# Own buffers for the strided heads, u^T of batch 1 in natural order, and a last step tile by tile

## The chip, the cores and the metric

The kernel runs on one core of one Trainium2 chip. The metric is device time in microseconds of one execution. The engines are PE (TensorE: matmuls and transpositions), DVE (VectorE), ACT (ScalarE), POOL (GpSimd) and SP (SyncE, which here only issues DMAs). ACT and POOL issue DMAs as well.

## The reference

For 8 batches, 8 heads, 576 positions and head size 64, attention is computed with two kinds of masks, and its output goes through a token-mixing and a channel-mixing layer:

```python
mask_local = (rel >= 0) & (rel < 32)                                       # heads 0 to 3
mask_strided = (rel >= 0) & (pos[None, :] % 32 == pos[:, None] % 32)       # heads 4 to 7
x = softmax(where(mask, q @ k.T / 8, -1e9)) @ v      # per head, put together to 576 x 512
u = x + (x.T @ U @ V).T                              # U: 576 x 32, V: 32 x 576
out = u + relu(u @ w_ch1) @ w_ch2                    # 512 -> 2048 -> 512
```

A strided head has 32 residue classes of 18 positions each, so its scores are 32 causal blocks of 18 x 18.

## The kernel before, in words

**The channel mixing sets the frame.** It runs over nine blocks n: the first 512 positions of batches 0 to 7, and a tail block (n = 8) of the last 64 positions of all eight batches. Each block has 16 steps fc over the 2048 inner columns. A step is `gemm1` (12 matmuls of 128 x 512 into one PSUM bank `ph`), then on ACT `gh` (relu) and on DVE `gl` (what rounding left of it), and `gemm2` (for each of four tiles s of 128 positions, two matmuls with `gh` and one with `gl`, into `accs[n]`). gemm2 of a step is issued behind gemm1 of the next step. The four tiles of `accs[n]` lie in two PSUM tiles of two banks each. `finish` adds x to the four tiles on DVE and sends them out. The two operands `uh` and `ul` of the next block are made by `split` from `raw`.

**The next batch's attention is woven in.** While block n runs, a generator `attention(n + 1)` is advanced along the 32 half-steps ("slots") of the block: local pairs of heads on PE (`scores`, `probabilities` with the tile `s_sb`, `transposed` with the tile `PT`, `outputs`), then the token mixing: `mix_t` (tile `ta`, result `tst`), `mix_u`, `mix_tail`, and `transposes`, which turns x on DVE into `bt` and spreads it into `raw` with 32 small DMAs, half issued by SP and half by ACT. From batch 2 on, `strided_heads(b)` computes the strided heads without PE: POOL multiplies (`tmp`), DVE sums (`tensor_reduce`), for the scores `s_st` (27 products and sums), then a softmax, then for the values (27 products and sums). The reduce of a product is traced one product later. `strided_copies` moves the result into x before the second half of `mix_t`.

**Batches 0 and 1 come first**, in `first_attention`: all heads as pairs on PE, the strided ones with positions sorted by residue class. Their output in class order (tile `x`) goes to DRAM through POOL's queue (`far_dma`), and `od_reads` brings it back in natural order into `xg`. u^T of a pair of heads is made by `quarter(b, pr)`: x transposed on PE into `pu`, U^T x into `pm`, V onto it, and for batch 1 copied to `raw`. For the strided pairs (pr 2 and 3) it takes the class order, with U and V sorted alike (`U_c`, `Vc`, `Vc_last`) and five instead of four pieces to transpose. The quarters of batch 1 run during block 0, in the order `ORDER1`.

**The shared buffers.** `att` gives tiles of one tag with `ATT_BUFS` = 5 buffers: `s_sb`, `PT`, `ta`, `h` of mix_tail, batch 1's `x` and `tst`, and also `s_st` and every `tmp` of the strided heads. During the prefix alone a list `ring` of eight pieces of the tiles `late` takes their place. A new tile waits until the one that had its buffer is read out.

**The order on each engine.** The kernel is traced as one program, and a planner orders each engine's instructions beforehand: it plays the program with costs of its own and gives an engine the first traced instruction that is ready. Work that is ready can so run ahead of its place in the program. On the chip each engine follows its order strictly. `tc.issue_after` adds an order on one engine. S0 and S1 give the slots over which the strided heads of a batch are traced.

Of the kernel before, what the change touches and what calls it, by code (L numbers as in the profile page):

```python
# [7 lines left out]
F32 = mybir.dt.float32  # L8
# [5 lines left out]
ALU = mybir.AluOpType  # L14
AX = mybir.AxisListType
NEG = -1.0e9
ATT_BUFS = 5
NSP = 2
N_EARLY = 9
N_LATE = 48  # L20
# [8 lines left out]
A_TAIL = (4, 20, 8)  # L29
S0 = {2: 20, **{b: 32 * (b - 1) - 12 for b in range(3, 8)}}  # L30
S1 = (20, 14)
ORDER0, ORDER1 = (2, 3, 0, 1), (2, 3, 0, 1)
PAIR = 2 * 576 + 18 * 65


# [1 line left out]
def fused_kernel(ctx, tc, pairs, strided, U, V, w_in, masks, eye, out):  # L37
# [67 lines left out]
    mask_l, ident_b = masks_sb[:, 0:320], masks_sb[:, 320:448]  # L105
    U_sb = const.tile([128, 5, R], F32, name="U_sb")
    Vst = const.tile([96, S], F32R, name="Vst")
    U_c = const.tile([128, 5, R], F32, name="U_c")
    Vc_last = const.tile([96, 64], F32R, name="Vc_last")
    uh, ul = (const.tile([128, NDC, 512], F32R, name=name) for name in ("uh", "ul"))  # L110
    raw = const.tile([128, 4, 4, NDC, 32], F32, name="raw")
# [21 lines left out]
    def small_weights():  # L133
        stage = xp.tile([128, 2, 512], I64, name="xg")
        words_in = stage.rearrange("p a x -> p (a x)")
        dma(out=words_in[:, 0:10 * R], in_=U)
        dma(out=words_in[0:R, 10 * R:10 * R + S], in_=V)
        yield
        with tc.issue_after(marks["PT"][0]):
            f = to_f32(words_in, early, 128, 10 * R)  # L140
        nc.scalar.copy(out=U_sb.rearrange("p t r -> p (t r)"), in_=f[:, 0:5 * R])
        nc.scalar.copy(out=U_c.rearrange("p t r -> p (t r)"), in_=f[:, 5 * R:10 * R])
        with tc.issue_after(marks["PT"][0]):
            f = to_f32(words_in[0:R, 10 * R:10 * R + S], att([128, 640], "cu"), R, S)
        nc.scalar.copy(out=Vst[0:32], in_=f)
        nc.scalar.copy(out=Vst[32:64], in_=f)
        nc.vector.tensor_tensor(out=Vst[64:96], in0=f, in1=Vst[0:32].bitcast(F32), op=ALU.subtract)
        yield
        by_class = Vst.bitcast(F32).rearrange("p (j c) -> p c j", j=NCH)
        nc.scalar.copy(out=Vc[:, 0:504].rearrange("p (c j) -> p c j", j=NCH), in_=by_class[:, 0:28])  # L150
        nc.scalar.copy(out=Vc[:, 504:512], in_=by_class[:, 28, 0:8])
        nc.scalar.copy(out=Vc_last[:, 0:10], in_=by_class[:, 28, 8:18])
        nc.scalar.copy(out=Vc_last[:, 10:64].rearrange("p (c j) -> p c j", j=NCH), in_=by_class[:, 29:32])
        yield
# [76 lines left out]
    def early_pair(b, pr, od, last):  # L231

        tb = 64 * (b % 2)
        by_class = pr >= 2
        kT, qT = load_qk(b, pr)
        yield
        vt = load_v(b, pr)
        yield
        before = marks.get("PV", [])
        with tc.issue_after(before[-1]) if before else nullcontext():  # L240
            sp = scores(kT, qT, mask_s if by_class else mask_l)
        s_sb = yield from probabilities(sp)
        load_behind(len(marks["exp"]) - 1, s_sb[0:1, 0, 0, 0:1])
        PT = transposed(s_sb)
        yield
        op = outputs(PT, vt)
        cs = slice(2 * pr * D, 2 * pr * D + 2 * D)
        if by_class:
            x = att5([128, 640], "x").rearrange("p (t x) -> p t x", t=5) if b else \
                early[:, 320 + 640 * (pr - 2):960 + 640 * (pr - 2)].rearrange("p (t x) -> p t x", t=5)  # L250
            main, last_x, p0 = x[:, 0:4, :], x[0:64, 4, :], 0
            normalised(op, x)
        else:
            xg, xt = x_tiles(b)
            main, last_x, p0 = xg[:, :, cs], xt[tb:tb + 64, cs], tb
            normalised(op, main, last_x, tb)
        if by_class:
            oc = 2 * pr * D - 4 * D
            far_dma(out=od[0:512, oc:oc + 2 * D].rearrange("(t p) d -> p t d", p=128), in_=main)
            far_dma(out=od[512:576, oc:oc + 2 * D], in_=last_x)  # L260
        parts[b, pr] = (main, last_x, p0)
        if last:
            od_reads(b, od)
        yield
        if b == 0:
            quarter(b, pr)
            yield

    def quarter(b, pr):

        main, last_x, p0 = parts[b, pr]
        by_class = pr >= 2
        cs = slice(2 * pr * D, 2 * pr * D + 2 * D)
        Um = U_c if by_class else U_sb
        pu = psx2().rearrange("p a x -> p (a x)")
        pm = ps_h.tile([128, 512], F32, name="ph")[0:32, 0:128] if b == 0 else pu[0:32, 640:768]
        lead = x_transposed(pu, [main[:, t, :] for t in range(4)])
        if by_class:
            lead = x_transposed(pu[:, 512:576], [last_x])
        with tc.issue_after(lead):  # L280
            for t in range(4):
                nc.tensor.matmul(pm, Um[:, t, :], main[:, t, :], start=t == 0 and not (b and by_class), stop=False,
                                 skip_group_check=True, tile_position=(0, 0))
            nc.tensor.matmul(pm, Um[p0:p0 + 64, 4, :], last_x, start=False, stop=True, skip_group_check=True,
                             tile_position=(p0, 0))
        if b not in tsts:
            tsts[b] = ap_.tile([96, DM], F32R, name="tst", **({"tag": "att", "bufs": ATT_BUFS} if b else {}))
        tst = tsts[b]
        nc.scalar.copy(out=tst[0:32, cs], in_=pm)
        nc.scalar.copy(out=tst[64:96, cs], in_=pm)  # L290
        nc.vector.tensor_tensor(out=tst[32:64, cs], in0=pm, in1=tst[0:32, cs].bitcast(F32), op=ALU.subtract)
        for c0, n, Vm in ((0, 512, Vc), (512, 64, Vc_last)) if by_class else ((0, 512, Vst),):
            nc.tensor.matmul(pu[:, c0:c0 + n], tst[:, cs], Vm[:, 0:n], start=False, stop=True, skip_group_check=True)
        src = pu[:, 0:512]
        if by_class:
            src = pu[:, 0:S].rearrange("p (c j) -> p j c", j=NCH)[:, 0:16, :]
        if b:
            dst = raw[:, :, :, pr, :]
            nc.scalar.copy(out=dst, in_=src.rearrange("p (s a) x -> p s a x", s=4) if by_class else
                           src.rearrange("p (s a x) -> p s a x", s=4, a=4))  # L300
        else:
            hi, lo = (u[:, pr, :].rearrange("p (j c) -> p j c", c=32) if by_class else u[:, pr, :] for u in (uh, ul))
            one = nc.scalar.copy(out=hi, in_=src)
            two = nc.vector.tensor_tensor(out=lo, in0=src, in1=hi.bitcast(F32), op=ALU.subtract)
            marks["split0"] = (two.ins, one.ins)
# [115 lines left out]
    def strided_heads(b):  # L421
# [3 lines left out]
        with tc.issue_after(marks["gl"][9]):  # L425
            dma(out=st, in_=strided[b - NSP, :, 0:2 * NCH * D])
        yield
        s_st = att([128, NCH, NCH], "s_st")
        nc.gpsimd.memset(s_st, 8.0 * NEG)
        late = []  # L430

# [4 lines left out]
        for i in range(NCH):  # L436
            for j0 in range(0, i + 1, 9):
                n = min(9, i + 1 - j0)
                tmp = att([128, 9, D], "tmp")
                nc.gpsimd.tensor_tensor(out=tmp[:, 0:n], in0=sk[:, j0:j0 + n], in1=sq[:, i:i + 1].broadcast_to([128, n, D]),  # L440
                                        op=ALU.mult)
                late.append(lambda tmp=tmp, n=n, i=i, j0=j0: nc.vector.tensor_reduce(  # L442
                    out=s_st[:, i, j0:j0 + n], in_=tmp[:, 0:n], axis=AX.X, op=ALU.add))
                flush(1)
                yield
# [17 lines left out]
        for i in range(NCH):  # L463
            step = D if i < 9 else D // 2
            for d0 in range(0, D, step):
                tmp = att([128, (i + 1) * step], "tmp")
                tv = tmp.rearrange("p (j d) -> p j d", d=step)
                nc.gpsimd.tensor_tensor(out=tv, in0=sv[:, 0:i + 1, d0:d0 + step],  # L468
                                        in1=s_st[:, i, 0:i + 1].broadcast_to([128, i + 1, step]), op=ALU.mult)
                late.append(lambda tv=tv, i=i, d0=d0, step=step: nc.vector.tensor_reduce(  # L470
                    out=o_st[:, i, d0:d0 + step], in_=tv.rearrange("p j d -> p d j"), axis=AX.X, op=ALU.add))
                flush(1)
                yield
# [184 lines left out]
        marks.setdefault("gl", []).append(low.ins)  # L658
        return gh, gl

    def gemm2(n, fc, gh, gl):
        if fc == 0:
            accs[n] = [ps_acc.tile([128, 2, 512], F32, name="acc") for _ in range(2)]
        for s in range(4):
            cs = slice(128 * s, 128 * s + 128)
            if fc == 0 and n < NSP:
                nc.tensor.matmul(accs[n][s // 2][:, s % 2, :], Vst[:, cs], tsts[n], start=True, stop=False)
# [1 line left out]
                nc.tensor.matmul(accs[n][s // 2][:, s % 2, :], gt[:, cs], w_parts[fc, 1][:, part, :],  # L669
                                 start=(fc == 0 and i == 0 and n >= NSP), stop=(fc == NFC - 1 and i == 2))  # L670

    def finish(n):
        for s in range(4):
            ot = xgs[n][:, s, :]
            nc.vector.tensor_tensor(out=ot, in0=accs[n][s // 2][:, s % 2, :], in1=ot, op=ALU.add)  # L675
            if n == B:
# [62 lines left out]
    for step, (n, fc) in enumerate(steps):  # L739
# [3 lines left out]
        advance(2 * step)  # L743
        if n == 0:
            convert(2 * upto[min(NFC - 1, fc + CLA)])
        if len(pend) > 1:
            item = pend.pop(0)
            gemm2(*item)
            if item[1] == NFC - 1:
                finish(item[0])  # L750
        advance(2 * step + 1)
    while pend:
        gemm2(*pend.pop(0))
    finish(NB - 1)


def _masks():
# [72 lines left out]
```

## Time and profile before

| | us |
|---|---|
| median of 3 runs (lowest to highest) | 940.63 (939.02 to 941.83) |
| profiled execution, its own time | 940.45 |
| its span | 938.7 |
| PE busy in the span | 909.2 |
| DVE, POOL, ACT busy | 561.6, 325.7, 247.2 |

An engine's busy time counts compute instructions. Block 0 begins at about 53 us, behind the first loads and the first heads; blocks 2 to 6 follow each other every 97.3 us. In a row of the timeline stand start, duration, engine, line, operation and tiles (out <- in), and in brackets the idle time before it with what ended it. "ACTq" and "SPq" are DMA issues on those engines. In the tables of windows stand the length of the window, the busy time and count of PE, PEld (weight loads), DVE, ACT and POOL, then the granted clock of PE, the DMA share and GB/s; a window asked for one line has fewer columns.

### The profile page before, as it was taken

The page shows a single profiled execution, that of the slowest core. Times are in us where ns is not written, and L with a number is a line of the kernel's source. Part 1 is how long each engine was busy: PE and PEld are TensorE (multiplying, and loading weights), DVE is VectorE, ACT ScalarE, POOL GpSimd, SP SyncE. Part 2 cuts the span into 40 slices and gives each one's busy share as a digit, 9 for nine tenths or more (in the row PEclk, how much of TensorE's full clock was granted, in tenths as well). Part 3 has the DMA queues.
Part 4 walks back from the last instruction along what each step waited for, and adds up shares of the span by engine and source line. Part 5 has one row for each costly group of instructions (what it writes and reads, how often), then busy time and mean ns, then how long its engine had stood idle before and what let it go on. Part 6 is the DMA issues. An engine that isn't in the chain of part 4 may idle for free.

```text
span 938.7 us, 16860 instructions
## 1 busy us (share of the span) xinstructions
PE 909.2 (97%) x7032; PEld 727.3 (77%) x7032; DVE 561.6 (60%) x907; ACT 247.2 (26%) x485; POOL 325.7 (35%) x374
## 2 busy tenths in 40 slices
PE   5789999999899999999999999999999999999997
PEld 4667888777677778777887788778877888888885
DVE  4679987757786678666776677657764341122111
ACT  4436542115122412151114221421233111121110
POOL 1213018434854385346644565447440000000000
PEclk9999999999989999999999999999999999999999
DMA  9958210200250114101420142013300231001001
GB/s 349 340 193 343 88 62 26 97 1 26 61 180 3 32 41 166 42 1 60 138 72 2 51 157 72 2 51 99 119 2 1 57 112 23 1 1 46 1 0 45
DMA packets 36780, 74.24 MB, mean 79 GB/s; under 512 B 5952, under 2 KB 20672, under 8 KB 34784
## 3 DMA queue, kind: packets, MB, share of 16 engines
q1 hardware_dynamic: 26464, 66.60, 20.1%
q10 hardware_dynamic: 9280, 4.20, 1.9%
q0 software_dynamic: 960, 2.36, 0.8%
q8 instruction: 55, 0.90, 0.4%
q14 instruction: 21, 0.17, 0.1%
HBM read 54.14 MB, written 11.67 MB: 70 GB/s over the span
## 4 chain that ended last, share of the span: by engine, by line
PE 83%; DVE 6%; POOL 5%; DMA 3%; issue 2%; ACT 1%; SPq 0%; DVEq 0%; POOLq 0%
PE acc L669 38%; PE ph L652 37%; POOL tmp L440 5%; DVE st L470 1%; PE px L380 1%; DMA w1a<-in_w_dram 1%; PE px L346 1%; PE px L367 1%; DMA w2a<-in_w_dram 1%; DMA late<-in_pairs_dram 1%; PE px L511 1%; DMA st<-in_strided_dram 1%; DVE gl L657 1%; PE px L534 1%; DVE s_st L442 0%
## 5 line engine op out<-in xcount | busy, mean ns | idle before, releaser
L657 DVE SCALAR_TENSOR_TENSOR gl<-ph,gh 128x512 fp32r<-128x512 f32 x144 | 98.8, 688 | 224.2 <-ACT gh L656 223.6
L652 PE MATMUL ph<-uh,w 128*128 128x512 f32 x648 | 215.0, 392 | 0.0
L656 ACT ACTIVATE gh<-ph 128x512 fp32r<-128x512 f32 x144 | 86.1, 598 | 471.2 <-PE ph L652 388.9
L440 POOL TENSOR_TENSOR tmp<-st 128x576 f32<-128x576 f32 (+6 forms) x162 | 168.7, 1082 | 114.0 <-DMA st<-in_strided_dram 58.3
L468 POOL TENSOR_TENSOR tmp<-st,s_st 128x448 f32<-128x448 f32 (+7 forms) x162 | 136.5, 873 | 183.7 <-DVE st L470 97.5
L669 PE MATMUL acc<-w,gh 128*128 128x512 f32 x648 | 197.6, 393 | 0.0
L470 DVE TENSOR_REDUCE st<-tmp 128x64 f32<-128x64 f32 (+8 forms) x162 | 137.6, 882 | 15.4 <-POOL tmp L468 14.3
L669 PEld LDWEIGHTS acc<-w,gh 128*128 128x128 f32 x648 | 122.2, 189 | 25.6
L652 PEld LDWEIGHTS ph<-uh,w 128*128 128x128 f32 x648 | 121.3, 188 | 26.4 <-issue 0.4
L652 PE MATMUL ph<-ul,w 128*128 128x512 f32 x324 | 126.8, 391 | 0.0
L669 PE MATMUL acc<-w,gl 128*128 128x512 f32 x324 | 122.2, 393 | 2.1 <-DVE gl L657 2.0
L442 DVE TENSOR_REDUCE s_st<-tmp 128x9 f32<-128x576 f32 (+6 forms) x162 | 87.6, 564 | 26.6 <-POOL tmp L440 25.7
L669 PEld LDWEIGHTS acc<-w,gl 128*128 128x128 f32 x324 | 61.4, 189 | 16.7 <-DVE gl L657 3.2
L652 PEld LDWEIGHTS ph<-ul,w 128*128 128x128 f32 x324 | 60.8, 188 | 12.9
L485 ACT COPY xg<-st 32x256 f32<-32x256 f32 x96 | 38.8, 404 | 8.5 <-DVE st L470 7.2
L522 DVE TENSOR_TENSOR ta<-px,ta 32x256 f32<-32x256 f32 x36 | 15.1, 420 | 33.1 <-ACT ta L520 32.3
L675 DVE TENSOR_TENSOR xg<-acc,xg 128x512 f32<-128x512 f32 x36 | 22.9, 681 | 9.3 <-PE acc L669 9.3
L644 DVE TENSOR_TENSOR ul<-raw,uh 128x512 fp32r<-128x512 f32 x32 | 24.7, 800 | 2.7 <-ACT uh L643 2.7
L652 PE MATMUL ph<-uh,w6a 128*128 128x512 f32 x72 | 25.1, 398 | 0.0
L652 PE MATMUL ph<-uh,w0a 128*128 128x512 f32 x72 | 24.8, 403 | 0.0
L652 PE MATMUL ph<-uh,w1a 128*128 128x512 f32 x72 | 24.1, 391 | 0.0
L652 PE MATMUL ph<-uh,w5a 128*128 128x512 f32 x72 | 23.8, 391 | 0.0
(292 smaller groups left out, 1272.4 us busy)
## 6 DMA issues: line engine op xcount, KB each, us to landing
w<-in_w_dram SPq DMA_DIRECT2D x9, 1024.0 KB, 8.6
out_dram<-xg SPq DMA_DIRECT2D x32, 256.0 KB, 2.1
v<-in_pairs_dram SPq DMA_DIRECT2D x12, 585.0 KB, 4.7
st<-in_strided_dram SPq DMA_DIRECT2D x6, 1152.0 KB, 5.6
qk<-in_pairs_dram SPq DMA_DIRECT2D x12, 576.0 KB, 5.1
late<-in_pairs_dram SPq DMA_DIRECT2D x8, 585.0 KB, 8.7
late<-in_pairs_dram SPq DMA_DIRECT2D x8, 576.0 KB, 9.7
raw<-bt SPq DMA_DIRECT2D x112, 32.0 KB, 1.9
```

Of the source, the lines that this page charges most:

```text
L440: nc.gpsimd.tensor_tensor(out=tmp[:, 0:n], in0=sk[:, j0:j0 + n], in1=sq[:, i:i + 1].broadcast_to([128, n, D]), op=ALU.mult)
L442: late.append(lambda tmp=tmp, n=n, i=i, j0=j0: nc.vector.tensor_reduce(out=s_st[:, i, j0:j0 + n], in_=tmp[:, 0:n], axis=AX.X, op=ALU.add))
L468: nc.gpsimd.tensor_tensor(out=tv, in0=sv[:, 0:i + 1, d0:d0 + step], in1=s_st[:, i, 0:i + 1].broadcast_to([128, i + 1, step]), op=ALU.mult)
L470: late.append(lambda tv=tv, i=i, d0=d0, step=step: nc.vector.tensor_reduce(out=o_st[:, i, d0:d0 + step], in_=tv.rearrange("p j d -> p d j" ...
L485: nc.scalar.copy(out=xg[32 * i4:32 * i4 + 32, :, cs], in_=o_st[rows, i4:16:4, :])
L522: nc.vector.tensor_tensor(out=ta, in0=ps_a[32 * j:32 * j + 32, :], in1=ta, op=ALU.add)
L644: nc.vector.tensor_tensor(out=lo, in0=raw[:, :, :, dc, :], in1=hi.bitcast(F32), op=ALU.subtract)
L652: nc.tensor.matmul(ph, w_parts[fc, 0][:, part, 128 * dc:128 * dc + 128], ut[:, dc, :], start=(dc == dcs[0] and i == 0), stop=(dc == dcs[-1 ...
L656: nc.scalar.activation(out=gh, in_=ph, func=AF.Relu)
L657: low = nc.vector.scalar_tensor_tensor(out=gl, in0=ph, scalar=0.0, in1=gh.bitcast(F32), op0=ALU.max, op1=ALU.subtract)
L669: nc.tensor.matmul(accs[n][s // 2][:, s % 2, :], gt[:, cs], w_parts[fc, 1][:, part, :], start=(fc == 0 and i == 0 and n >= NSP), stop=(fc ...
L675: nc.vector.tensor_tensor(out=ot, in0=accs[n][s // 2][:, s % 2, :], in1=ot, op=ALU.add)
```

## The change

Three parts:

1. `s_st` and `tmp` of the strided heads get tags of their own, one buffer for `s_st` and three of 128 x 576 for `tmp`; `ATT_BUFS` goes from 5 to 2. To make room `U_c` moves into a free part of the tile `late[0]`.
2. Batch 1's strided quarters read the natural order (`xg` and the tail tile, as brought back by `od_reads`) with `U_sb` and `Vst`, as the local quarters do, and `ORDER1` puts them last.
3. In the last block the gemm2 of step 14 is held back, and steps 14 and 15 are done together by tiles: tiles 0 and 1 of both steps and their `finish`, then tile 2, then tile 3.

```diff
-ATT_BUFS = 5
+ATT_BUFS = 2
-ORDER0, ORDER1 = (2, 3, 0, 1), (2, 3, 0, 1)
+ORDER0, ORDER1 = (2, 3, 0, 1), (0, 1, 2, 3)
...
-    U_c = const.tile([128, 5, R], F32, name="U_c")
...
-        nc.scalar.copy(out=U_c.rearrange("p t r -> p (t r)"), in_=f[:, 5 * R:10 * R])
+        nc.scalar.copy(out=late[0][:, 1816:1816 + 5 * R], in_=f[:, 5 * R:10 * R])
...
             far_dma(out=od[512:576, oc:oc + 2 * D], in_=last_x)
+            if b:
+                xg, xt = x_tiles(b)
+                main, last_x, p0 = xg[:, :, cs], xt[tb:tb + 64, cs], tb
...
-        by_class = pr >= 2
+        by_class = pr >= 2 and b == 0
-        Um = U_c if by_class else U_sb
+        Um = late[0][:, 1816:1816 + 5 * R].rearrange("p (t r) -> p t r", r=R) if by_class else U_sb
...
-        s_st = att([128, NCH, NCH], "s_st")
+        s_st = ap_.tile([128, NCH, NCH], F32, name="s_st")
...
-                tmp = att([128, 9, D], "tmp")
+                tmp = ap_.tile([128, 9, D], F32, name="tmp", tag="tmp", bufs=3)
...
-                tmp = att([128, (i + 1) * step], "tmp")
-                tv = tmp.rearrange("p (j d) -> p j d", d=step)
+                tmp = ap_.tile([128, 9 * D], F32, name="tmp", tag="tmp", bufs=3)
+                tv = tmp[:, 0:(i + 1) * step].rearrange("p (j d) -> p j d", d=step)
...
-    def gemm2(n, fc, gh, gl):
+    def gemm2(n, fc, gh, gl, tiles=range(4)):
-        for s in range(4):
+        for s in tiles:
...
-    def finish(n):
-        for s in range(4):
+    def finish(n, tiles=range(4)):
+        for s in tiles:
...
-        if len(pend) > 1:
+        if len(pend) > 1 and step + 1 < len(steps):
...
-    while pend:
-        gemm2(*pend.pop(0))
-    finish(NB - 1)
+    for tiles in ((0, 1), (2,), (3,)):
+        for item in pend:
+            gemm2(*item, tiles=tiles)
+        finish(NB - 1, tiles)
```

More of the change, by code (lines that the diff above doesn't have):

```diff
@@ L281, in quarter @@
             for t in range(4):
-                nc.tensor.matmul(pm, Um[:, t, :], main[:, t, :], start=t == 0 and not (b and by_class), stop=False,
+                nc.tensor.matmul(pm, Um[:, t, :], main[:, t, :], start=t == 0, stop=False,
                                  skip_group_check=True, tile_position=(0, 0))
@@ L298, in quarter @@
             dst = raw[:, :, :, pr, :]
-            nc.scalar.copy(out=dst, in_=src.rearrange("p (s a) x -> p s a x", s=4) if by_class else
-                           src.rearrange("p (s a x) -> p s a x", s=4, a=4))
+            nc.scalar.copy(out=dst, in_=src.rearrange("p (s a x) -> p s a x", s=4, a=4))
         else:
```

## The prediction

> **What bounds the kernel now.** I read the page's first part, then the table of windows, then the chain of waits, then each engine's timeline where the windows showed a hole.
>
> ```profile
> PE 909.2 (97%) x7032; PEld 727.3 (77%) x7032; DVE 561.6 (60%) x907; ACT 247.2 (26%) x485; POOL 325.7 (35%) x374
> 250.00:300.00 50.00, 45.48 (x402) 35.37 (x400) 37.23 (x63) 8.59 (x15) 28.20 (x31) 0.93 0.31 101
> 300.00:350.00 50.00, 50.00 (x321) 39.72 (x320) 33.95 (x55) 16.81 (x40) 27.24 (x29) 1.00 0.11 32
> ```
>
> PE is the bound (first busy column). In the middle of the run it has one large hole, 4.52 us in 250 to 300, where the granted clock (third number from the end) is 0.93; the window behind it is full, as are those after. POOL and DVE are never full, so faster strided heads pay only where they close that hole. Its size is seen in the first-layer matmuls that open blocks 1, 2 and 3:
>
> ```profile
> L652 PE MATMUL ph<-uh,w1a x8: 388/389/389, 167.8 to 170.3; 128*128 128x512 f32 x8
> L652 PE MATMUL ph<-uh,w1a x8: 388/389/389, 274.7 to 277.2; 128*128 128x512 f32 x8
> L652 PE MATMUL ph<-uh,w1a x8: 388/389/389, 372.0 to 374.5; 128*128 128x512 f32 x8
> 924.29 2.72 PE ph L652 x12
> ```
>
> Block 2 takes 372.0 - 274.7 = 97.3 us and block 1 takes 106.9, which is 9.6 more. The last row is a step of the chain: twelve matmuls in 2.72, 0.227 each. Block 1 has four matmuls more (V times tst in gemm2), 0.9. So 8.7 us are lost. Where:
>
> ```profile
> 173.14 0.50 PE L669 MATMUL acc<-w0b,gl 128*128 128x512 f32 x1 [0.63 <-DVE gl L657]
> 247.43 0.40 PE L652 MATMUL ph<-uh,w 128*128 128x512 f32 x1
> 247.71 6.33 ACTq L98 DMA_DIRECT2D raw<-bt  x8
> 254.15 0.60 ACT L656 ACTIVATE gh<-ph 128x512 fp32r<-128x512 f32 x1 [11.56 <-DMA raw<-bt]
> 255.93 0.43 PE L340 MATMUL px<-masks_sb 128*128 128x320 bf16 x2 [2.43 <-DVE xt L549]
> 259.81 0.79 PE L669 MATMUL acc<-w,gl 128*128 128x512 f32 x1 [1.98 <-DVE gl L657]
> 256.50:263.30 6.80, 4.82 (x12) 3.31 (x11) 4.19 (x7) 0.60 (x1) 6.80 (x6) 0.50 0.24 58
> 346.73 0.60 ACT L656 ACTIVATE gh<-ph 128x512 fp32r<-128x512 f32 x1 [4.85 <-DMA raw<-bt]
> 346.75 4.61 ACTq L98 DMA_DIRECT2D raw<-bt  x7
> ```
>
> A step's gh is due when its matmuls end, here at 247.83. ACT's queue had eight DMA issues of the transposes ahead of it. They could start only at 247.71, and gh came at 254.15, 6.3 late. Between a step's matmuls and its gemm2 lie one gemm2 and one gemm1, 2 x 2.72 = 5.44 us; less 0.60 for gh and about as much again for gl, some 4.1 are spare. So PE starved, twice, and ran at half clock for 6.8 us (4.82 busy, so 2.4 lost). In block 2 seven such issues start 0.02 behind a gh and hurt nobody: the queue's order is the same, only the transposes of block 1 were late. What made them late is batch 2's strided heads:
>
> ```profile
> 91.64 0.92 POOL L440 TENSOR_TENSOR tmp<-st 128x64 f32<-128x64 f32 x1
> 95.68 0.70 POOL L440 TENSOR_TENSOR tmp<-st 128x128 f32<-128x128 f32 x1 [3.11 <-PE px L284]
> 137.90 23.84 POOL L440 TENSOR_TENSOR tmp<-st 128x192 f32<-128x192 f32 x22 [41.53 <-DVE xt L549]
> 137.85 0.41 DVE L442 TENSOR_REDUCE s_st<-tmp 128x1 f32<-128x64 f32 x2
> 177.54 1.13 POOL L468 TENSOR_TENSOR tmp<-st,s_st 128x64 f32<-128x64 f32 x3 [8.03 <-DVE s_st L459]
> 196.73 0.73 POOL L468 TENSOR_TENSOR tmp<-st,s_st 128x320 f32<-128x320 f32 x1 [10.86 <-DVE st L470]
> 201.97 3.11 POOL L468 TENSOR_TENSOR tmp<-st,s_st 128x352 f32<-128x352 f32 x4 [3.42 <-PE px L367]
> 177.50:230.50 53.00, 53.00 (x472) 41.73 (x470) 33.60 (x49) 15.35 (x35) 23.40 (x28) 1.00 0.01 2
> 228.12 2.35 DVE L470 TENSOR_REDUCE st<-tmp 128x32 f32<-128x576 f32 x2
> 322.82 1.20 DVE L470 TENSOR_REDUCE st<-tmp 128x32 f32<-128x576 f32 x1
> ```
>
> Products wait for things that have nothing to do with strided heads: 95.68 for a quarter's matmul (its tile x), 137.90 for mix_tail's add (its tile h), 201.97 for a transposition (its tile s_sb). That is the shared ring of five. The last reduce ends at 230.47; in block 2 at 324.02, which is 217.1 on block 1's clock (106.9 earlier). Batch 2 is 13.4 us late.
>
> **The change, part by part.**
>
> *Buffers of their own.* No instruction is added. First half (scores): the first reduce runs on DVE at 137.85 although its product was ready at 92.56, so DVE's order, not the buffer, held it; three products instead of two are ahead then, which saves one, about 0.6, and POOL, without a pause from 137.90 to 161.74, remains the limit. I take nothing. Second half (values): it starts at 177.54 behind the softmax, which stays. The window to 230.50 has 33.60 us of DVE and 23.40 of POOL work. Without any gap DVE ends at 211; if half of its 19.4 idle us stay, at 221. So the last reduce comes 9 to 19 us earlier, about where block 2 has it. To save the first starvation the eight issues must end within the spare time, by 247.83 + 4.1 = 251.9, thus begin at 245.6, only 2.1 earlier. So the stall should go. Block 1 then costs 97.3 + 0.9 + the 0.63 wait at 173.14, which is other DVE work and stays: 98.8 for 106.9, a gain of 8.1. Bounds: 8.7 if that wait goes too, 0 if nothing moves.
>
> *Two shared buffers for the rest.* h, batch 1's x and tst, s_sb, PT and ta now share two. Both x are free once written out, ahead of the read at 70.97 below. tst of batch 1 keeps one until gemm2's first step of block 1 is through (the row at 173.14 is in it); the first s_sb of batch 2 is written behind that step, so s_sb and PT find both free. Cost 0; if PT had to wait, the local pair would be late by a step of 5.44. U_c inside late[0]: that tile is kept by later heads anyway, so weight 8's load is not later. 0.
>
> *Quarters from natural order.* Two quarters lose two of ten transposing instructions and a 64-column matmul each.
>
> ```profile
> 80.69 0.47 PE L667 MATMUL acc<-tst,Vst 96*128 96x512 f32 x1 [0.72 <-DVE xt L396]
> 108.09 1.05 PE L316 MATMUL px<-ident,xg 128*128 128x128 f32 x8
> 70.97 2.21 POOL L101 DMA_DIRECT2D xg<-od  x4 [4.96 <-DMA od<-x]
> ```
>
> Eight cost 1.05, so two cost 0.26. The first of the two quarters stood just ahead of a 0.72 wait for DVE and only lengthens it, so I count one: 0.3 (bounds 0 and 0.6). The strided quarters now need what GpSimd's queue reads back from 70.97 on, but as third and fourth of the order they come at 108 or later: 30 us of cover. Without it PE would wait for a DMA of some us.
>
> *Last two steps tile by tile.*
>
> ```profile
> 930.48 0.39 PE L669 MATMUL acc<-w,gl 128*128 128x512 f32 x1
> 931.16 0.61 PE L669 MATMUL acc<-w,gl 128*128 128x512 f32 x2
> 931.58 2.48 DVE L675 TENSOR_TENSOR xg<-acc,xg 128x512 f32<-128x512 f32 x4 [3.21 <-PE acc L669]
> 932.06 0.39 PE L669 MATMUL acc<-w,gl 128*128 128x512 f32 x1
> 932.31 2.76 ACTq L98 DMA_DIRECT2D out_dram<-xg  x4
> DMA to landing us min/median/max: 2.4/3.0/3.4
> ```
>
> Now the four adds run from 931.58 to 934.06. From 927.01 (924.29 + 2.72) the new order does twelve matmuls for tiles 0 and 1 (to 929.73), six for tile 2 (931.09), whose add ends near 931.75, and six for tile 3. The first add now starts when the matmul at 931.16 ends (931.55), not behind the one at 930.48 that ended at 930.87: the wait is for the whole two-bank accumulator. If tile 3's matmuls, in the same accumulator, wait likewise for tile 2's add, they run 931.75 to 933.11 and the last add ends at 933.75, 0.3 earlier. The last rows then leave on empty queues and land as the fastest here do, 2.4 and not 3.4: 1.0 more. I take 1.3. Without that wait the add ends at 933.1 and the gain is 2.0; with the crowded landing it is 0.3.
>
> The Trainium skill's "PSUM — Partial Sum Buffer", section "Summary: rules for kernel authors", says to read PSUM during matmuls from a different bank and to guard by bank; by it tile 3 need not wait, and the sum below would be 930.1 for 930.8. The rows at 930.48 to 931.58 speak for the wait, so I keep it.
>
> Sum, against the profiled execution's 940.45 (span 938.7; the median of the runs is 940.63, 0.18 above): 940.45 - 8.1 - 0.3 - 1.3 = 930.75, say 930.8.
>
> **Rivals.** (a) *The strided heads do not move.* POOL's longest wait in the second half, 10.86, is put down to DVE's reduce, not to a shared tile, and the first reduce lay ready for 45 us. If DVE's planned order is the limit, only the ends pay: 940.45 - 0.3 - 1.3 = 938.9. Against it: the plan places a reduce by when its product can exist, and that hung on the ring.
>
> (b) *Half of the stall stays.* The second group of eight still meets a due gh: one wait of 2.43 and the 2.4 of half clock remain, so 4.8 of 8.1: 940.45 - 3.3 - 1.6 = 935.6. The Trainium skill's "TensorE: Matmul & The Clock Gate", Part 1, has the clock fall to half after an idle window of about 3.4 us; by that rule waits of 2.43 leave it whole and (b) gives 933.2. The row 256.50:263.30 shows 0.50 without so long a wait, so it disagrees.
>
> (c) *Slower: the DMA issues meet gh in later blocks.* Blocks 2 to 6 now escape by 0.02 us (346.73 and 346.75). If reduces that leave DVE sooner move the transposes within the step, eight issues can come just ahead of a due gh in each: 6.33 - 4.1 = 2.2 each at least, 8.7 as in block 1 at most. Two blocks at 8.7, or five at 2.2, eat the gain. At 4 in each of five: 930.8 + 20 = 950.8. Against it: the transposes follow mix_u's matmuls, and PE, full there, runs those at their place in the program however early the heads are.
>
> **How the numbers follow.** Forecast 0.57, (a) 0.14, (b) 0.12, (c) 0.13, slower for a reason that I do not see 0.04. A difference under 0.3% (2.8 us) is about what this measurement cannot tell from none: below 937.8 is faster, forecast and (b), 0.69; (a) is the same, 0.14; slower 0.17. The forecast's own range is 928 (block 1 at 8.7, tail 2.0, quarters 0.6 make 929.2, less the 1 us by which runs differ) to 934 (tail 0.3, block 1 two or three us short). The range for 8 in 10 adds (b) and (a): 928 to 940.5; left out is 0.17.
>
> **What would show it.** Right: w1a of block 2 begins 98 to 99 us after that of block 1; no PE hole in 240 to 265 and granted clock 1.00 there; the last reduce of batch 2 before 222; no product waits for px, h or x; last add near 933.7. Wrong: POOL still waits some 10 us for L470 and the last reduce ends after 228; or PE holes beside ACT's issues in later blocks.

## The result and the profile after

The changed kernel takes 991.12 us (989.60 to 992.36), the kernel before 940.24 (939.02 to 941.83) on the same chip: a ratio of 1.0539, 95% interval 1.0517 to 1.0562, some 50 us slower. The profiled execution of the changed kernel took 990.63, its span is 988.8. Forecast were 930.8. The experiments below ran on several chips, each beside the kernel before, whose median there was 939.83 to 940.84. Of the ten executions of `e9_tmp_ring` one took 1012.63 at a granted clock of 0.854 and is not in its ratio.

From the page after, the busy times and the granted clock in 40 slices (here a slice is 24.7 us):

```profile
PE 928.9 (94%) x7026; PEld 735.9 (74%) x7026; DVE 569.0 (58%) x907; ACT 246.6 (25%) x485; POOL 330.8 (33%) x374
...
PEclk9697899999999999999999999999999999999999
```

PE is busy for 928.9 us where it was 909.2, with nearly the same matmuls (7026 records for 7032): a part of them ran at a lower clock, and the clock is low in the first five slices. So the first loss is ahead of block 1. The matmuls that open blocks 1, 2 and 3 (before: 167.8, 274.7, 372.0):

```profile
L653 PE MATMUL ph<-uh,w1a x8: 388/389/390, 199.7 to 202.2; 128*128 128x512 f32 x8
L653 PE MATMUL ph<-uh,w1a x8: 388/389/389, 303.8 to 306.3; 128*128 128x512 f32 x8
L653 PE MATMUL ph<-uh,w1a x8: 388/389/390, 406.7 to 409.1; 128*128 128x512 f32 x8
```

Prefix and block 0 lose 199.7 - 167.8 = 31.9 us. Block 1 takes 104.1, 2.8 less than before. Block 2 takes 102.9 for 97.3, and blocks 3 to 5 lose about as much each, 21 in all for the four; behind them nothing more is lost. 31.9 - 2.8 + 21 = 50.1, the difference of the spans.

**The first loss.** The instructions of one tile, the products `tmp`, in 20 to 130 us of the changed kernel (count, duration in ns, first and last start):

```profile
L441 POOL TENSOR_TENSOR tmp<-st x27: 313/1254/1777, 24.8 to 61.7; 128x576 f32<-128x576 f32 x11, 128x64 f32<-128x64 f32 x2, 128x128 f32<-128x128 f32 x2, 128x192 f32<-128x192 f32 x2
L443 DVE TENSOR_REDUCE s_st<-tmp x27: 208/601/753, 25.1 to 63.2; 128x9 f32<-128x576 f32 x11, 128x1 f32<-128x64 f32 x2, 128x2 f32<-128x128 f32 x2, 128x3 f32<-128x192 f32 x2
L469 POOL TENSOR_TENSOR tmp<-st,s_st x27: 304/928/1500, 71.5 to 120.4; 128x320 f32<-128x320 f32 x3, 128x384 f32<-128x384 f32 x3, 128x448 f32<-128x448 f32 x3, 128x512 f32<-128x512 f32 x3
L471 DVE TENSOR_REDUCE st<-tmp x27: 220/918/1232, 71.8 to 124.7; 128x32 f32<-128x320 f32 x2, 128x32 f32<-128x352 f32 x2, 128x32 f32<-128x384 f32 x2, 128x32 f32<-128x416 f32 x2
```

All 54 products and 54 sums of batch 2's strided heads now stand between 24.8 and 126, where all but the first two products ran from 137.9 on before, in the middle of batches 0 and 1 and of the weights' conversion. The table of windows from 20 to 165 us, first of the kernel before, then of the changed one:

```profile
20.00:165.00 145.00, 136.74 (x1520) 108.28 (x1521) 118.16 (x186) 65.85 (x107) 44.61 (x66) 0.99 0.50 180
```

```profile
20.00:165.00 145.00, 114.68 (x1375) 87.73 (x1376) 138.73 (x207) 59.78 (x105) 76.44 (x95) 0.86 0.47 171
```

DVE (third busy column) is at 138.73 of 145 us; PE (the first) falls from 136.74 to 114.68.

**The second loss.** Rows of DVE, ACT and PE in block 1 of the changed kernel, and the window behind PE's wait; blocks 2 to 5 repeat them:

```profile
263.09 3.27 DVE L471 TENSOR_REDUCE st<-tmp 128x32 f32<-128x384 f32 x4
266.40 0.42 DVE L523 TENSOR_TENSOR ta<-px,ta 32x256 f32<-32x256 f32 x1
266.74 0.97 DVE L471 TENSOR_REDUCE st<-tmp 128x32 f32<-128x448 f32 x1
267.75 0.42 DVE L523 TENSOR_TENSOR ta<-px,ta 32x256 f32<-32x256 f32 x1
268.10 0.97 DVE L471 TENSOR_REDUCE st<-tmp 128x32 f32<-128x448 f32 x1
269.10 0.43 DVE L523 TENSOR_TENSOR ta<-px,ta 32x256 f32<-32x256 f32 x1
269.46 0.96 DVE L471 TENSOR_REDUCE st<-tmp 128x32 f32<-128x480 f32 x1
270.45 0.69 DVE L658 SCALAR_TENSOR_TENSOR gl<-ph,gh 128x512 fp32r<-128x512 f32 x1
```

```profile
262.77 0.60 ACT L657 ACTIVATE gh<-ph 128x512 fp32r<-128x512 f32 x1 [1.90 <-PE ph L653]
269.56 0.40 ACT L525 CAST tst<-ta 32x256 fp32r<-32x256 f32 x1 [6.20 <-DVE ta L523]
269.99 0.40 ACT L526 CAST tst<-ta 32x256 fp32r<-32x256 f32 x1
270.42 0.60 ACT L657 ACTIVATE gh<-ph 128x512 fp32r<-128x512 f32 x1
```

```profile
271.19 0.50 PE L670 MATMUL acc<-w,gl 128*128 128x512 f32 x1 [1.77 <-DVE gl L658]
```

```profile
271.20:275.50 4.30, 4.26 (x12) 3.09 (x13) 4.27 (x5) 0.00 (x0) 2.92 (x4) 0.65 0.00 0
```

The value sums of the next batch (L471) alternate with mix_t's sums (`ta`). The `gl` that PE waits for is the one of 270.45. Its `gh` is that of 262.77, since no other `gl` stands between the two, and that `gh` came as soon as its matmuls ended. It was done at 263.37, so `gl` stood 7.1 us behind other work in DVE's order, seven value sums (6.2 us) among it. PE waits 1.77; then it runs 4.3 us at a clock of 0.65. The same wait (1.76 or 1.77) comes once in each of blocks 1 to 5.

ACT is held back too: its copies of `tst` wait 6.20 for `ta`, and the `gh` of 270.42 is queued behind them. But that `gh` belongs to the next step, whose `gl` PE takes up at 278.66 without a wait, so here it costs nothing. Over the whole run the waits of ACT for `ta` show how far DVE's order pushed mix_t back, first in the changed kernel, then before:

```profile
ACT tst L525 <- DVE ta L523: 72.4, 12, 8.1
```

```profile
ACT tst L524 <- DVE ta L522: 14.9, 7, 4.5
```

**The end.** The adds of the changed kernel (before: four from 931.58, ended at 934.06):

```profile
980.95 1.89 DVE L676 TENSOR_TENSOR xg<-acc,xg 128x512 f32<-128x512 f32 x3 [2.53 <-PE acc L670]
984.58 0.69 DVE L676 TENSOR_TENSOR xg<-acc,xg 128x512 f32<-128x512 f32 x1 [1.75 <-PE acc L670]
```

The last add ends at 985.27, 8.38 behind the start of the last two steps' gemm2 (976.89); before it was 7.21 (926.85 to 934.06). From there to the end of the span it is 3.5, before 4.6. So the end gains nothing.

### The profile page after: what moved, and what is told of

Same layout as the page of the kernel before. It is cut to its first block, busy times and chain, and to the rows that moved or that the text cites. A ratio compares the mean times of both kernels' runs of the same rounds, so it can differ in the third digit from the quotient of the medians.

```text
span 988.8 us, 16802 instructions
## 1 busy us (share of the span) xinstructions
PE 928.9 (94%) x7026; PEld 735.9 (74%) x7026; DVE 569.0 (58%) x907; ACT 246.6 (25%) x485; POOL 330.8 (33%) x374
## 4 chain that ended last, share of the span: by engine, by line
PE 54%; DVE 19%; POOL 15%; DMA 6%; ACT 4%; issue 1%; SPq 0%; ACTq 0%; POOLq 0%; DVEq 0%
PE acc L670 26%; PE ph L653 24%; POOL tmp L441 14%; DVE st L471 8%; DMA st<-in_strided_dram 4%; ACT xg L486 3%; DVE gl L658 2%; DVE s_st L443 1%; DVE ta L523 1%; DMA out_dram<-xg 1%; POOL tmp L469 1%; DVE xg L676 1%; PE px L535 1%; DMA xg<-in_U_dram 1%; DVE cv L128 1%
## 5 line engine op out<-in xcount | busy, mean ns | idle before, releaser
L658 DVE SCALAR_TENSOR_TENSOR gl<-ph,gh 128x512 fp32r<-128x512 f32 x144 | 98.8, 686 | 251.7 <-ACT gh L657 250.9
L670 PE MATMUL acc<-w,gh 128*128 128x512 f32 x648 | 201.3, 397 | 1.8 <-DVE xg L676 1.8
L469 POOL TENSOR_TENSOR tmp<-st,s_st 128x448 f32<-128x448 f32 (+7 forms) x162 | 140.2, 890 | 59.7 <-DVE st L471 32.2
L471 DVE TENSOR_REDUCE st<-tmp 128x64 f32<-128x64 f32 (+8 forms) x162 | 135.7, 866 | 6.3 <-POOL tmp L469 5.0
L670 PE MATMUL acc<-w,gl 128*128 128x512 f32 x324 | 125.5, 404 | 9.3 <-DVE gl L658 8.8
L443 DVE TENSOR_REDUCE s_st<-tmp 128x9 f32<-128x576 f32 (+6 forms) x162 | 90.4, 570 | 63.9 <-POOL tmp L441 63.5
L653 PE MATMUL ph<-uh,w3a 128*128 128x512 f32 x72 | 24.5, 402 | 1.1 <-DVE gl L658 1.1
L653 PE MATMUL ph<-uh,w4a 128*128 128x512 f32 x72 | 25.4, 401 | 0.0
L670 PE MATMUL acc<-w2b,gh 128*128 128x512 f32 x72 | 22.8, 400 | 2.5 <-ACT gh L657 1.9
L645 DVE TENSOR_TENSOR ul<-raw,uh 128x512 fp32r<-128x512 f32 x32 | 20.4, 687 | 6.6 <-ACT uh L644 6.5
```

The costliest lines, as they stand in the source:

```text
L645: nc.vector.tensor_tensor(out=lo, in0=raw[:, :, :, dc, :], in1=hi.bitcast(F32), op=ALU.subtract)
L653: nc.tensor.matmul(ph, w_parts[fc, 0][:, part, 128 * dc:128 * dc + 128], ut[:, dc, :], start=(dc == dcs[0] and i == 0), stop=(dc == dcs[-1 ...
L658: low = nc.vector.scalar_tensor_tensor(out=gl, in0=ph, scalar=0.0, in1=gh.bitcast(F32), op0=ALU.max, op1=ALU.subtract)
```

## The experiments

Theory 1: the shared ring of five was a brake. The planner places an instruction as early as its data and its buffer allow; with buffers of their own it puts the strided heads where DVE is full. (The expectations say that the value sums stand ahead of mix_t's sums; the rows above show that `gl`, behind both, is what PE waits for.) "Held" below means tied behind an instruction of DVE in DVE's order. Rival 2 is the two buffers left for the rest or the quarters, rival 3 that products and sums which no longer wait slow the engines wherever they stand.

**Batch 2's score sums held** (`e1_hold_first`):

```
+        hold = marks["gl"][-1] if b == NSP else None
         def flush(n):
             while len(late) > n:
-                late.pop(0)()
+                with tc.issue_after(hold) if hold is not None else nullcontext():
+                    late.pop(0)()
```

> The changed kernel, with the 27 score sums of batch 2 alone tied behind the gl of the step in which they are traced (step 10 of block 0), so that they cannot be ordered into the prefix. Theory 1 (the shared ring of five was a brake: without it the planner orders batch 2's strided heads into the prefix, which gives 31.9 of the 50.5 us, and in blocks 1 to 5 it puts the next batch's value sums ahead of mix_t's sums on DVE, which gives the rest): w1a of block 1 starts at 168 +-2 as before, blocks 2 to 5 stay at 102.5 each, and the time is 991.1 - 31.9 = 959, 956 to 962. Rival 2 (the prefix lost its time to the two buffers left for the rest, or to the quarters from natural order): w1a of block 1 stays above 190 and the time above 982.

Measured: 964.04 (961.30 to 966.78), ratio 1.0248 (1.0201 to 1.0295). The openings of blocks 1 and 3:

```profile
L655 PE MATMUL ph<-uh,w1a x8: 388/389/389, 170.0 to 172.5; 128*128 128x512 f32 x8
...
L655 PE MATMUL ph<-uh,w1a x8: 388/389/389, 382.9 to 385.4; 128*128 128x512 f32 x8
```

Block 1 opens at 170.0 where it was 199.7: the first loss is batch 2's strided work in the prefix, with quarters and buffers as in the changed kernel, so rival 2 is out. The median of the two executions lies some 2 us above the expected range; they are 5.5 apart, and the slower one is profiled. In it blocks 1 and 2 took 212.9, more than in the changed kernel (207.0), probably because batch 2's values now also stand in block 1.

**All score sums held** (`e2_hold_all`): `hold = marks["gl"][-1]` for every batch.

> The changed kernel, with the 27 score sums of every batch tied behind the gl of the step in which they are traced (step 10 of the block two ahead). Theory 1: prefix as before, blocks 2 to 5 back at 97.3 each (21 us less than in the kernel with batch 2 alone held), and block 1 at 98 to 100 instead of 106.9 since the sums of batch 2 no longer share the ring: 930 to 934. If the prediction's gain in block 1 does not exist: 938 to 940. Rival 3 (products and sums that run without waiting for the ring slow the other engines wherever they stand): blocks 2 to 5 above 100 and the time above 950.

Measured: 941.04, ratio 1.0001 (0.9988 to 1.0013). The openings of blocks 1 and 3 (of the second the first three), then all of PE's waits from 240 us on (the second row is in the last steps):

```profile
L655 PE MATMUL ph<-uh,w1a x8: 388/389/389, 166.6 to 169.1; 128*128 128x512 f32 x8
...
L655 PE MATMUL ph<-uh,w1a x3: 388/389/389, 363.1 to 364.4; 128*128 128x512 f32 x3
```

```profile
PE acc L672 <- DVE gl L660: 3.2, 3, 1.1
PE acc L672 <- DVE xg L678: 1.8, 1, 1.8
```

Same instructions, same buffers, another order on DVE: all 50 us are gone, and rival 3 with them. Blocks 1 and 2 took 196.5 for 204.2 (forecast 196.1). But the time is no better than before: blocks 3 to 7 took 6.9 more than before and gave the gain back. A part of that is three waits of about 1.1 at the end of every other block, where the last score sum waits for its product with a due `gl` behind it in DVE's order.

**Value sums held instead** (`e3_hold_values`): score sums held for batch 2 alone; at the start of the value half `hold = marks["gl"][-1]`.

> The changed kernel, with the score sums held for batch 2 alone, and the 27 value sums of every batch tied behind the gl of the step in which they are traced (step 0 of the next block), so that from batch 3 on it is the score sums that stand beside mix_t. Theory 1 in its narrow form (it is the value sums, some 0.87 us each and 23 us in a row, that hold back mix_t's sums): blocks 2 to 5 at 97 to 98, 930 to 940. In its wide form (whatever strided sums stand beside mix_t's cost the step): blocks 2 to 5 at 100 or more, 945 to 960. Rival 3: above 950 as well, but with DVE slowed in its single instructions and not waited for in its order.

Measured: 954.87, ratio 1.0143 (1.0116 to 1.0171). ACT in block 2:

```profile
333.77 0.41 ACT L528 CAST tst<-ta 32x256 fp32r<-32x256 f32 x1 [7.11 <-DVE ta L526]
334.20 0.40 ACT L529 CAST tst<-ta 32x256 fp32r<-32x256 f32 x1
334.63 0.60 ACT L660 ACTIVATE gh<-ph 128x512 fp32r<-128x512 f32 x1
```

The wide form holds: score sums beside mix_t make ACT wait for `ta` as value sums do, and blocks 2 to 5 take 101 to 104. What counts is that strided sums stand there in DVE's order, not the length of the single sum.

**The ring again** (`e4_shared_ring`): `ATT_BUFS = 5`, and `s_st` and `tmp` from `att(...)`; quarters and end as in the change.

> The first part undone: strided heads and the rest share the ring of five again; quarters of batch 1 from natural order and the last steps tile by tile stay. Theory 1: prefix, block 1 (107 us with its hole) and blocks 2 to 5 as before; quarters -0.3 and the end about 0 (in the changed kernel the last add ends 1.2 us later, seen from the last first-layer matmul, and the landing is 1.1 us shorter): 939.5 to 940.5. The prediction's two terms would give 938.9. Rival 2 in its form that the quarters cost the prefix: above 960.

Measured: 941.07, ratio 1.0009 (0.9992 to 1.0025). Block 1 opens as before:

```profile
L653 PE MATMUL ph<-uh,w1a x8: 388/389/389, 165.1 to 167.6; 128*128 128x512 f32 x8
```

The buffers carry the whole loss. Quarters and end together are worth nothing that shows; the prediction's 938.9 (a ratio of 0.9983) lies outside the interval.

**Which half fills the prefix** (`e5_no_sums`, `e8_no_products`). The first leaves out batch 2's 54 sums:

```
             while len(late) > n:
-                late.pop(0)()
+                one = late.pop(0)
+                if b > NSP:
+                    one()
```

> The changed kernel without the 54 sums of batch 2's strided heads on DVE (its output for that batch is left unsummed); the 54 products stay on POOL, and stay in the prefix, ahead of the same gate copies and transfers. Theory 1a (in the prefix it is DVE that was overrun: sums stand in its order ahead of conversions, normalisations and splits): w1a of block 1 at 168 +-2, later blocks as in the changed kernel, time 957 to 962. Rival 1b (POOL: weight gates and the od transfers wait in its queue behind products, or products on POOL slow DVE's two-input operations): w1a of block 1 above 190, time above 980. In between: the share is read from where it lands.

The second leaves out batch 2's 54 products; its sums read `st` as it stands (the edit for the scores, that for the values is alike):

```
+                if b == NSP:
+                    tmp = sk[:, j0:j0 + n]
+                else:
                     nc.gpsimd.tensor_tensor(out=tmp[:, 0:n], ...)
```

> The other half of the run without sums: the changed kernel without batch 2's 54 products on POOL (its sums read q, k and v as they stand, so that batch's strided output is not the reference's); the 54 sums stay on DVE, and stay in the prefix. After the run without sums, products alone gave the whole loss, by DVE instructions that ran up to 7.9 us beside them where 0.9 is usual. Theory 1a (sums alone also give it: some 38 us more in DVE's order, ahead of the conversions): w1a of block 1 at 190 to 203, time 980 to 992. Theory 1b (it is the products that cost, through DVE's longer instructions; sums fill DVE's idle time): w1a of block 1 at 166 to 175, time 957 to 966.

Measured: 989.23, ratio 1.0524 (1.0499 to 1.0549), and 989.25, ratio 1.0514 (1.0479 to 1.0549). Either half alone gives the whole first loss. In theory 1a and 1b each half was to exclude the other; both fell in that form. Products without sums, from the windows of that run and its timelines of DVE and POOL:

```profile
20.00:165.00 145.00, 112.35 (x1362) 86.42 (x1363) 129.00 (x148) 59.83 (x103) 69.01 (x95) 0.88 0.49 175
```

```profile
49.88 7.93 DVE L128 SCALAR_TENSOR_TENSOR cv<-w2a,cv 128x512 int32<-128x512 int32 x1
```

```profile
49.90 7.37 POOL L443 TENSOR_TENSOR tmp<-st 128x576 f32<-128x576 f32 x6
```

Sums without products:

```profile
20.00:165.00 145.00, 109.29 (x1372) 85.25 (x1373) 126.99 (x210) 61.73 (x106) 18.36 (x41) 0.87 0.48 175
```

Without sums nothing makes the products pause, and some DVE instructions with operands in SBUF alone last as long as a string of products: the one above 7.93 us, where its shape takes 0.69. Nine such instructions take 38.9 us in this window; by the durations that the same shapes have in `e1_hold_first` they would take 6.5. So DVE loses 32 us, and block 1 opens at 201.6, 31.6 later than in `e1_hold_first`. Without products DVE does 37.1 us of sums ahead of due work, and block 1 opens at 199.4. In the changed kernel, sums (38.3) and products pace each other, and few instructions are stretched (four by over 1 us, to 2.6 at most). The delay also falls elsewhere: without products block 0 opens at 86.5, so the whole loss lies ahead of it, where in the changed kernel it opens at 66.2 and before at 55.9. In all three it is DVE that has over 30 us more to do where it had no room; that the two do not add up is read from the traces, and no further run tells them apart. Nor was the rest of rival 1b, weight gates and transfers that queue behind products on POOL, tested by itself.

**Which buffer was the brake** (`e9_tmp_ring`): `ATT_BUFS = 4`, `tmp` from `att(...)`, `s_st` with its own buffer.

> Half of the first part undone: the products share a ring (of four) with h, x, tst, s_sb, PT and ta again, while the scores s_st keep a buffer of their own. Theory 1 in the form that the products' own three buffers took the brake away: prefix, block 1 and later blocks as before, 938 to 942. If it was the scores' own buffer (in the kernel before s_st could be set only when the ring came free for it): the prefix still loses, 960 to 992.

Measured: 939.34, ratio 0.9986 (0.9971 to 1.0002). The score sums of batch 2 (up to 165 us):

```profile
L443 DVE TENSOR_REDUCE s_st<-tmp x26: 209/612/756, 132.7 to 163.9; 128x9 f32<-128x576 f32 x10, 128x1 f32<-128x64 f32 x2, 128x2 f32<-128x128 f32 x2, 128x3 f32<-128x192 f32 x2
```

They are back at 132.7. It was the products' share of the ring that held the strided heads in their place, not the tile of the scores.

**Earlier, later, and paced** (`e6_hold_late`, `e7_pace_late`). Both hold the score sums one step earlier, and trace batch 2 later. The first does the last two steps in two pairs of tiles; the second also paces the value sums and orders the end by hand, with tile 3 in a PSUM tile of its own (its end is left out here):

```
-S0 = {2: 20, ...}
+S0 = {2: 22, ...}                 # 24 in e6_hold_late
+        hold = marks["gl"][-1 if b == NSP else -2]
...
-                late.pop(0)()
+                with tc.issue_after(hold or marks["gl"][-2]):
+                    late.pop(0)()
...
         o_str[b] = o_st
+        hold = None                # e7_pace_late alone
```

> As the kernel with all score sums held, but one step earlier (behind the gl of step 9) for batches 3 to 7, two steps later for batch 2 (traced from slot 24), and with the last two steps in two pairs of tiles, (0, 1) and (2, 3). Theory 1: what that kernel gave back in blocks 2 to 6 (three waits of gl of 1.2 at a block's end and 1.75 in the score matmuls of the local pairs) came from sums that began at 64.8 of a block where the kernel before began at 58.5; one step earlier the gl waits go: 941 - 3.6 - about 1 at the end = 935 to 938. Rival 4 (the value sums, 27 in a row at the block's start, are what costs): no better than 939 to 941.

> As the kernel with score sums held one step earlier, batch 2 from slot 22; besides, each value sum is tied behind the gl of the step before the one in which it is traced, so that they spread over a block's first seven steps; and the last two steps are ordered by hand (tiles 0 to 2 of step 15, 0 and 1 of step 16, tile 3 of step 15, then 2 and 3), with tile 3 in a PSUM tile of its own. Theory 1 with theory 5 (the tail's gain was lost to the wait for the shared PSUM tile and to the planner's order): blocks 2 to 5 at 97.3 to 97.8, block 1 at 98 to 100, and the last add ends 6.3 behind the last first-layer matmul (8.4 in the changed kernel, 7.2 before): 931 to 934. Rival 4: 97.3 here and 98 or more without the pacing. If theory 5 is wrong, the end stays at 90.7 or more from w1a of the tail block to the end of the span.

Measured: 938.31, ratio 0.9987 (0.9971 to 1.0003), and 932.28, ratio 0.9918 (0.9903 to 0.9932). The first moved the waits, but holding the scores better was not enough; its 938.3 lies between what theory 1 and rival 4 expected. With the value sums spread as well, the openings of blocks 1 and 3 of `e7_pace_late`, batch 2's value sums in block 1, and all of PE's waits from 166 to 840 us are:

```profile
L656 PE MATMUL ph<-uh,w1a x8: 388/389/389, 166.5 to 169.0; 128*128 128x512 f32 x8
...
L656 PE MATMUL ph<-uh,w1a x8: 388/389/389, 362.8 to 365.3; 128*128 128x512 f32 x8
```

```profile
L474 DVE TENSOR_REDUCE st<-tmp x27: 220/912/1224, 176.5 to 210.3; 128x32 f32<-128x320 f32 x2, 128x32 f32<-128x352 f32 x2, 128x32 f32<-128x384 f32 x2, 128x32 f32<-128x416 f32 x2
```

```profile
PE px L341 <- DVE xt L397: 0.7, 3, 0.2
```

Blocks 1 and 2 take 196.3 together for 204.2: 7.9 us. No `gl`, `ta` or transfer is waited for. (Blocks are taken in twos here: the opening matmul stands a little earlier or later against the rest of its step in every other block of this order.) The end was not what theory 5 expected: tile 1 lies in one PSUM tile with tile 0, and its matmuls waited for tile 0's add:

```profile
922.04 0.73 PE L678 MATMUL acc<-w,gh 128*128 128x512 f32 x2 [0.78 <-DVE xg L686]
```

**The end, tile by tile without that wait** (`e10_pace_end`):

```
-    for x, tiles in (... (1, (0,)), (1, (1,)), (0, (3,)), (1, (2,)), (1, (3,))):
+    for x, tiles in (... (1, (0, 1)), (0, (3,)), (1, (2,)), (1, (3,))):
```

> The paced kernel with one change in its last steps: tiles 0 and 1 are finished together (tile 1's last matmuls waited 0.78 for tile 0's add, since both lie in one PSUM tile), then 2 and 3, each in a PSUM tile of its own. Theory 5 (the wait is for the whole PSUM tile): the last add ends 6.35 behind the last first-layer matmul, 1.1 earlier than in the paced kernel: 931.2. If the landing eats it: 932.3, as the paced kernel.

Measured: 933.04, ratio 0.9914 (0.9899 to 0.9928). First the start of the last steps' gemm2 on PE, then the adds:

```profile
918.64 0.62 PE L678 MATMUL acc<-w,gh 128*128 128x512 f32 x2
```

```profile
922.24 2.05 DVE L686 TENSOR_TENSOR xg<-acc,xg 128x512 f32<-128x512 f32 x3 [2.08 <-PE acc L678]
924.28 0.69 DVE L686 TENSOR_TENSOR xg<-px,xg 128x512 f32<-128x512 f32 x1
```

The last add ends 6.33 behind 918.64, as expected with tiles 2 and 3 in PSUM tiles of their own (7.42 in the paced kernel). The landing behind it takes 4.3 for 3.9, so 0.7 of the 1.1 us is left in the trace; the times (0.9914 and 0.9918) do not tell the two kernels apart.

**Pacing without buffers** (`e11_pace_ring`): the same with `ATT_BUFS = 5` and `s_st`, `tmp` from `att(...)`.

> The paced kernel with its new end, but with strided heads and the rest in the ring of five again: pacing and end without the buffers. If the buffers are what block 1 gains from (the prediction's first term): block 1 and 2 together stay near 204 as in the kernel before, and only the end pays (some 0.7): 939 to 941. If the pacing alone does it (batch 2 traced a step later, sums behind a gl): blocks 1 and 2 together at 196 to 198, and 932 to 934 without any buffer of their own.

Measured: 938.21, ratio 0.9986 (0.9969 to 1.0002). The openings of blocks 1 and 3, and the window in which the kernel before had its hole:

```profile
L656 PE MATMUL ph<-uh,w1a x8: 388/389/389, 167.5 to 170.0; 128*128 128x512 f32 x8
...
L656 PE MATMUL ph<-uh,w1a x8: 388/389/389, 372.1 to 374.6; 128*128 128x512 f32 x8
```

```profile
240.00:265.00 25.00, 19.25 (x76) 14.92 (x75) 19.49 (x35) 1.79 (x3) 24.69 (x23) 0.86 0.16 43
```

204.6 for both blocks, with PE at 19.25 of 25 and a clock of 0.86: the hole is still there. The 7.9 us need the buffers; the pacing only keeps them from being lost elsewhere. The paced kernel (932.28, or 933.04 with the other end) is 0.8% faster than the kernel before, and some 59 us faster than the changed one.

## Why the prediction was wrong

**Buffers of their own, first half: this is the step that failed.** The term was set to nothing, and for blocks 2 to 5 the sum has no term at all. "DVE's order, not the buffer, held it ... I take nothing." DVE's order did hold the first sum at 137.85, but that order was the planner's, and it hung on the ring of the products (`e9_tmp_ring`: with the products back in a ring the first sum is at 132.7, without it at 25.1). That the planner placed the sum by its product is argued; its own times are not on record. The question what else the planner would do with freed instructions was not asked. It cost 31.9 us in the prefix and, by value sums ahead of a due `gl`, 21 in blocks 2 to 5. Rival (a) had the right sentence in it ("the plan places a reduce by when its product can exist, and that hung on the ring") and used it only for the gain.

**Second half: right in size, and covered; the path was only in part the one described.** Forecast was 98.8 us for block 1, a gain of 8.1. Block 1 takes 98.7 where DVE's order is kept (`e2_hold_all`), blocks 1 and 2 together gain 7.9 in `e7_pace_late`, and that gain hangs on the buffers (`e11_pace_ring`). As described, the strided heads end earlier and the transposes follow: in block 1 ACT issues the first of them at 237.81 in `e7_pace_late`, at 247.71 before and at 247.80 in `e11_pace_ring`.

That the last value sum of `e7_pace_late` begins at 210.3, beside the forecast 211 for its end, is luck: there the sums are spread over seven steps by hand. In `e2_hold_all`, where they are not, the last one begins at 196.4.

The hole itself was misread. PE never waited for the late `gh`. Its waits of 2.43 and 1.98 end, by rows that the prediction shows, with DVE's `xt` and with a `gl`. That `gl` ran 4.3 us after its `gh` was done (254.75), behind score sums that waited for their products:

```profile
257.03 0.55 DVE L442 TENSOR_REDUCE s_st<-tmp 128x6 f32<-128x384 f32 x1 [0.22 <-POOL tmp L440]
258.40 0.75 DVE L442 TENSOR_REDUCE s_st<-tmp 128x9 f32<-128x576 f32 x1 [0.81 <-POOL tmp L440]
259.07 0.68 DVE L657 SCALAR_TENSOR_TENSOR gl<-ph,gh 128x512 fp32r<-128x512 f32 x1
```

DVE waited for nothing of ACT's from 247.60 to there, so an earlier `gh` would not have moved this `gl`. It was DVE's order that starved PE before the change too, and in the changed kernel the same thing, a `gl` behind strided sums, costs blocks 1 to 5 a wait each. No run changed ACT's order alone. In the changed kernel 2.8 of the gain were left, since batch 3's sums stood ahead of `gl` in the same block.

**Rival (c)** had the loss in later blocks and nearly its price (20 us for five blocks, where 21 fell on four). But the price was not paid to DMA issues: ACT's wait for transfers of `raw` ahead of `gh` fell from 77.3 to 42.3 us. PE waited for a `gl` that stood behind sums in DVE's order while its `gh` was in time. That the price came near is luck. The argument against (c), that the transposes follow PE's place in the program, says nothing of DVE's order and so did not help.

**Two shared buffers for the rest**, taken at 0: no wait of PE falls on them in the paced kernel. **Quarters**, taken at 0.3, and **the end**, at 1.3: together nothing measurable (`e4_shared_ring`). The end's step had the landing right (1.0 forecast, 1.1 measured) and the kind of tile 3's wait for tile 2's add, but not its size (0.7 forecast, 1.75 measured). What it missed is that the planner moved the last `gl` matmul of tiles 0 and 1 behind tile 2's `gh` ones, so that no add ran early; the last add ended 1.2 later instead of 0.3 earlier.

**The signs named.** "No product waits for px, h or x" and the last reduce of batch 2 before 222 (at 126) came true and meant nothing; w1a of block 2 came 104 us after block 1's, not 98 to 99.

## What to carry to other kernels

Where a scheduler places work by readiness, a shared buffer is also a brake: before it is taken away, ask of every instruction that becomes ready earlier where it will be placed and which engine is full there, the prologue first. If a brake goes, put an explicit order in its place, here two ties behind a `gl` on DVE. And where an engine's order is fixed, work that nobody waits for can stand ahead of work that is due: here 6.2 us of sums ahead of a `gl` of 0.7. When PE waits for such an instruction, compare its start with the end of its own input before blaming the input. Busy shares of DVE of 58 to 60% over the run show nothing of either loss; short windows do, such as the 138.73 of 145 us above.

## What the runs showed of the hardware

A DVE instruction with its operands in SBUF could last as long as a string of POOL products: 7.93 us beside six products (49.90 to 57.27) in `e5_no_sums`, where its shape takes 0.69, though the record has it begin 0.02 ahead of them. Eight others in the window from 20 to 165 us took 2.4 to 6.4 us. It is not always the whole string: beside four products from 110.30 on, four such instructions took 1.1 to 1.4 us each. In the same window the groups that read PSUM kept their durations (`gl` 0.68). The Trainium skill's "SBUF — State Buffer", section "Who interferes with whom", has a DVE instruction with two SBUF inputs contend with a GpSimd instruction that reads SBUF, and calls the shared pair of ports an exclusive lock; the blocking agrees, but here one instruction of DVE stood behind up to six of POOL.

After a wait of PE of 1.77 us the clock was 0.65 for the next 4.3 us; after one of 1.06 it stayed at 1.00, in a window of the same length (`e2_hold_all`, from 457.3). The length of the wait alone does not decide it: behind the wait of 1.75 in the last steps of the changed kernel the clock was 1.00 too (982.89 to 985.00, when the last matmul is done).
